# Half-width tap matrices on TensorE and a reordered opening in a fused convolution and feed-forward kernel

## The chip, the cores and the metric

The kernel runs on one core of one Trainium2 chip. The metric is the device time of one launch in microseconds. Before the change the median of 9 runs is 699.56 us (698.77 to 700.28).

## The reference

A depthwise causal convolution of 7 taps along the sequence, with softmax-normalised taps for each of 8 heads, is followed by a feed-forward layer with a leaky ReLU. Cut to what matters:

```python
# x: (8, 4096, 192) float32, weight: (8, 7), w_in: (192, 2048), w_out: (2048, 192)
w = np.exp(weight - np.max(weight, axis=-1, keepdims=True))
w = w / (np.sum(w, axis=-1, keepdims=True) + 1e-09)
x_pad = np.concatenate([np.zeros((B, 6, D)), x], axis=1)
out = np.einsum('hk,bskhg->bshg', w, x_unf)   # x_unf[b, s, k] = x_pad[b, s + k], 24 columns per head
h = out.reshape(B * S, D) @ w_in
y = np.maximum(0.01 * h, h) @ w_out           # (32768, 192) float32
```

## The kernel before

**Tiling.** Two batch rows (e = 0, 1) are worked on together. A block is 512 positions of both rows; there are 32 blocks. The 192 columns are cut into three chunks of 64. A tile such as xt or yt holds, for each chunk, 64 columns of row 0 on partitions 0 to 63 and 64 columns of row 1 on partitions 64 to 127, and positions along the free axis. The first five blocks are worked on in halves of 256 positions, ten of them ("half 0" to "half 9"), and the other blocks whole. The list `groups` (lines 64 and 65) holds these ten halves and then the blocks.

**Bringing x in.** The first four halves come by SyncE in float32 (load_first, tile x_nat, two buffers), are cast to bf16 (cast_first, tile x_bf), transposed on TensorE (transpose_first, two tiles ptr in PSUM) and copied out of PSUM (evac_first) into xt. The later blocks come by load_x (six cast DMAs on GpSimd's queue into x_bf, three buffers) and transpose_x (three transposing DMAs on SyncE's queue).

**The convolution.** VectorE does it with one TENSOR_SCALAR (line 168) and six SCALAR_TENSOR_TENSOR (line 174) for each chunk, giving yt. For chunks 0 and 1 of halves 0 and 1 TensorE does it in its place (pe_conv_jobs, line 190): for each tap a diagonal matrix of the tap weights, in two parts (a bf16 value and the rest), is multiplied with the shifted xt and summed in a PSUM tile acc; the sum is scaled by the softmax's denominator on the way out. The diagonal matrices (tile diag, 128 by 128) are made by VectorE (the high part, line 274) and ScalarE (the low part, line 282).

**The two products.** mm1 multiplies yt with 128 columns of w_in at a time into ph (PSUM pool with 2 buffers of two banks), and ScalarE applies the leaky ReLU into g (line 348). A step j of a half is two such u. The second product is cut into slots, of which mm2_slot works one: each slot is one 128-row chunk of w_out for one unit of 128 positions of one row, half of its rows now and the other half LAG = 24 slots later. So unit n starts in slot 16n, is complete in slot 16n + 39, and is then copied out by evac_o (line 400) and stored by SyncE, two units at a time.

**PSUM.** The tiles ptr, acc and po share one tag of a pool with 4 buffers of one bank each.

**The order.** The kernel is written under a manual schedule: on each engine and each queue the instructions stand in the order of the program. The main loop runs over the groups i; within it the steps j: two mm1, then `quota` slots of the second product (none in half 0, 16 in each step of half 1 and later halves), then the convolution instructions of the next group (`ahead`), and then what stands at special places. Before the main loop stand the loads of weights, the softmax of the taps, the warming products (warm, line 236, on zeros), the tap matrices and the convolution of half 0. These lines set the places of halves 1 to 3:

```python
if i == 0 and u == 1:            # half 1: transposes and copies, then the conv of half 1
    transpose_first(1)
...
if i < 2 and j == 3:
    transpose_first(i + 2)
    evac_first(i + 2, nc.vector.tensor_copy, nc.vector.tensor_copy)
```

Of the kernel before, what the change touches and what calls it, by code (L numbers as in the profile page):

```python
# [9 lines left out]
FP32 = mybir.dt.float32  # L10
BF16 = mybir.dt.bfloat16
# [3 lines left out]
def kernel(  # L15
# [8 lines left out]
    nc = tc.nc  # L24
# [10 lines left out]
    CH = 64  # L35
# [34 lines left out]
    def load_x(blk):  # L70

        if blk >= NBLK:
            return
        rp, st = divmod(blk, NB)
        t = xb_pool.tile([128, NCH, SUB, 2, CH], BF16, name="x_bf")
        src = x[:, st * ST : (st + 1) * ST, :].rearrange("r (s p) d -> r p s d", p=128)
        for c in range(NCH):
            for e in range(2):
                nc.gpsimd.dma_start(  # L79
                    out=t[:, c, :, e, :],  # L80
                    in_=src[2 * rp + e, :, :, c * CH : (c + 1) * CH],
                )
# [21 lines left out]

    def load_first(q):
        t = stage_pool.tile([128, 2, HS, D], FP32, name="x_nat")
        for e in range(2):
            nc.sync.dma_start(  # L110
                out=t[:, e, :, :],
                in_=x[e, q * HT : (q + 1) * HT, :].rearrange("(c p) d -> p c d", p=128),
            )
        x_nat[q] = t

    def cast_first(q, e, copy):
# [27 lines left out]
    def evac_first(q, *copies):  # L144
        dst = xt[0][:, :, HALO + q * HT : HALO + (q + 1) * HT].rearrange(
            "p c (s i k) -> p i s c k", s=HS, i=2
        )
        for i, t in enumerate(ptr.pop(q)):
            copies[i](out=dst[:, i], in_=t)  # L149
# [4 lines left out]
    def conv_jobs(grp, chunks=range(NCH)):  # L154
        blk, t0, T = grp
        rp, st = divmod(blk, NB)
        if blk not in yt:
            yt[blk] = yt_pool.tile([128, NCH, ST], BF16, name="yt")
        y = yt[blk]
        jobs = []  # L160
        for c in chunks:
            for k in range(K):
                a = BASE + k + st * ST + t0
                src = xt[rp][:, c, a : a + T]
                dst = y[:, c, t0 : t0 + T]
                if k == 0:
                    jobs.append(
                        lambda s=src, d=dst, c=c: nc.vector.tensor_scalar_mul(  # L168
                            d, s, wk[:, c, 0:1]
                        )  # L170
                    )
                else:
                    jobs.append(
                        lambda s=src, d=dst, c=c, k=k: nc.vector.scalar_tensor_tensor(  # L174
                            out=d, in0=s, scalar=wk[:, c, k : k + 1], in1=d,
                            op0=mybir.AluOpType.mult, op1=mybir.AluOpType.add,
                        )
                    )
        return jobs

    def pe_conv_jobs(grp, c):


        blk, t0, T = grp
        acc = psum_o.tile([128, ST], FP32, name="acc", tag="po")
        jobs = []
        for p in range(2):
            for k in range(K):
                jobs.append(
                    lambda k=k, p=p: nc.tensor.matmul(  # L190
                        out=acc[:, :T], lhsT=diag[c][:, p, k, :],
                        rhs=xt[0][:, c, BASE + k + blk * ST + t0 : BASE + k + blk * ST + t0 + T],
                        start=(k == 0 and p == 0), stop=(k == K - 1 and p == 1),
                    )
                )
        return jobs, lambda scale: scale(yt[blk][:, c, t0 : t0 + T], acc[:, :T], rsum[:, c, :])  # L196


# [8 lines left out]
    nc.vector.memset(junk, 0.0)  # L207
    ident = const_pool.tile([128, 128], BF16)
    make_identity(nc, ident)

    sel = const_pool.tile([H, NCH, 2, CH], FP32, name="sel")
    nc.gpsimd.memset(sel, 1.0)  # L212
# [21 lines left out]
    def warm(n):  # L234
        for _ in range(n):
            nc.tensor.matmul(  # L236
                out=wa[:, 0, 0:HT], lhsT=zero[:, 0:128], rhs=zero, start=True, stop=True
            )
# [9 lines left out]
        out=w9[:, 0:K], in_=w9[:, 0:K], func=mybir.ActivationFunctionType.Exp,  # L248
        bias=nmax, scale=1.0, accum_out=w9[:, K : K + 1],
    )  # L250
    warm(7)
    wps = psum_h.tile([128, 2, ST], FP32, name="wps", tag="ph")
    for c in range(NCH):
        nc.tensor.matmul(
# [7 lines left out]
    cast_first(0, 1, nc.scalar.copy)  # L262

    wraw = wps[:, 0, 0 : NCH * (K + 1)].rearrange("p (c k) -> p c k", c=NCH)
    wkh = const_pool.tile([128, NCH, K], BF16, name="wkh")
    wkl = const_pool.tile([128, NCH, K], FP32, name="wkl")
    nc.vector.tensor_copy(out=wkh, in_=wraw[:, :, 0:K])
    nc.vector.tensor_sub(wkl, wraw[:, :, 0:K], wkh)


    diag = [const_pool.tile([128, 2, K, 128], BF16, name=f"diag{c}") for c in range(NPEC)]

    def diag_high(c):
        nc.vector.tensor_mul(  # L274
            diag[c][:, 0],
            ident[:, None, :].to_broadcast([128, K, 128]),
            wkh[:, c, :, None].to_broadcast([128, K, 128]),
        )

    def diag_low(c, ks):  # L280
        for k in ks:
            nc.scalar.activation(  # L282
                out=diag[c][:, 1, k, :], in_=ident,
                func=mybir.ActivationFunctionType.Copy, scale=wkl[:, c, k : k + 1],
            )

    transpose_first(0)
    warm(3)
    diag_high(0)
    diag_low(0, range(2))  # L290
    evac_first(0, nc.vector.tensor_copy, nc.scalar.copy)
    diag_low(0, range(2, K))
    diag_high(1)
    diag_low(1, range(K))
    rsum = const_pool.tile([128, NCH, 1], FP32)
# [7 lines left out]
            out=out, in_=in_, func=mybir.ActivationFunctionType.Copy, scale=scale  # L303
        )

    load_first(2)
    for job in conv_jobs(groups[0], range(NPEC, NCH)):
        job()
    for c in range(NPEC):
# [5 lines left out]
    cast_first(1, 0, nc.vector.tensor_copy)  # L315
    cast_first(1, 1, nc.vector.tensor_copy)
    load_first(3)
    load_x(2)
    transpose_x(2)


    g, po, osb, seal = {}, {}, {}, {}
# [70 lines left out]
    def evac_o(n):  # L393
# [7 lines left out]
        if n % 2 == 1:  # L401
# [3 lines left out]
                in_=osb.pop(n // 2),  # L405
            )

    slot, avail = 0, 0
    for i, grp in enumerate(groups):
        blk, t0, T = grp  # L410
        steps = T // 64
        if t0 == 0:
            g[blk] = g_pool.tile([128, NFC, 2, ST], BF16, name="g", tag="g")
        quota = (avail - slot) // steps

        if i == 0:
            ahead, pe_ahead = [], []
# [81 lines left out]
```

## Time and profile before

| | us |
|---|---|
| median of 9 runs | 699.56 |
| the profiled execution, device time | 698.8 |
| its span, first to last instruction | 697.1 |
| TensorE busy (share of the span) | 689.7 (99%) |
| VectorE busy | 540.3 (78%) |
| ScalarE busy | 512.2 (73%) |
| GpSimd busy | 142.0 (20%) |
| VectorE's SCALAR_TENSOR_TENSOR rows of the convolution | 439.5 |
| TensorE's tap products (56) | 7.6 |
| ScalarE's low tap matrices (14) | 4.3 |
| VectorE's high tap matrices (2) | 2.2 |

Busy times come from one profiled execution. Matmuls overlap, and their ends are modelled, so a busy TensorE is not TensorE at its peak. In the timelines a row gives the start, the length, the engine (PE is TensorE, PEld its weight loads, DVE VectorE, ACT ScalarE, POOL GpSimd, SP SyncE; a q after it means its queue), the line, the operation, the tile written and those read, the shapes and the count; in brackets stands how long the engine was idle before it and what ended that.

### The profile page before, as it was taken

To read this page: it belongs to the slowest core of one execution; us is meant where nothing else is said; L and a number is where in the kernel's file an instruction comes from. 1 tells how busy PE (TensorE), PEld (TensorE's weight loads), DVE (VectorE), ACT (ScalarE), POOL (GpSimd) and SP (SyncE) were. 2 spreads that over 40 slices of the span, in tenths; PEclk is the share of its full clock that TensorE was granted. 3 is DMA by queue.
4 is the path that set the end of the run, shared out by engine and by line. 5 is a ranking of instruction groups with operands and counts; after the bars stand their busy time and mean duration, and the time that the engine had idled before them with its cause. 6 is when DMAs were issued, how large, how long until landed. Compare 5 with 4: busy or idle time off the path is not lost.

```text
span 697.1 us, 25946 instructions
## 1 busy us (share of the span) xinstructions
PE 689.7 (99%) x11730; PEld 611.7 (88%) x11730; DVE 540.3 (78%) x995; ACT 512.2 (73%) x574; POOL 142.0 (20%) x198
## 2 busy tenths in 40 slices
PE   9999999999999999999999999999999999999997
PEld 6899998678888888888888888888888888888887
DVE  6799999967777787777787777787777787777712
ACT  6788887977777777777777777777777777777770
POOL 6432221420222211222220222211222210000000
PEclk9999999999999999999999999999999999999999
DMA  9986653855556635557644556525555535112112
GB/s 177 129 93 74 83 84 70 91 71 81 73 66 93 81 65 87 66 74 93 79 75 78 70 72 89 85 64 82 73 75 84 87 67 76 55 51 59 47 36 69
DMA packets 184847, 54.37 MB, mean 78 GB/s; under 512 B 148385, under 2 KB 184737, under 8 KB 184737
## 3 DMA queue, kind: packets, MB, share of 16 engines
q0 software_dynamic: 98768, 14.17, 29.4%
q1 hardware_dynamic: 85968, 38.56, 22.7%
q8 instruction: 91, 1.49, 0.9%
q14 instruction: 20, 0.16, 0.1%
HBM read 29.88 MB, written 25.17 MB: 79 GB/s over the span
## 4 chain that ended last, share of the span: by engine, by line
PE 89%; DVE 6%; DMA 3%; issue 0%; ACT 0%; POOL 0%; POOLq 0%; ACTq 0%
PE po L361 46%; PE ph L341 44%; DVE yt L174 6%; DMA w_out<-in_moe_w_out_dram 2%; DMA w_in<-in_moe_w_in_dram 1%; DVE yt L168 0%; ACT g L348 0%; POOL sel L214 0%; DVE xt L149 0%; POOL sel L212 0%; PE ptr L135 0%; DVE o_sb L400 0%; POOL ident masks.py:199 0%; ACT o_sb L400 0%; POOL ident masks.py:197 0%
## 5 line engine op out<-in xcount | busy, mean ns | idle before, releaser
L348 ACT ACTIVATE g<-ph 128x1024 bf16<-128x1024 f32 x512 | 496.2, 1021 | 165.3 <-PE ph L341 165.3
L174 DVE SCALAR_TENSOR_TENSOR yt<-xt,wk,yt 128x512 bf16<-128x512 bf16 (+1 forms) x642 | 439.5, 685 | 17.4
L361 PE MATMUL po<-w_out,g 64*128 64x192 bf16 (+1 forms) x8048 | 397.8, 243 | 0.2 <-DMA w_out<-in_moe_w_out_dram 0.2
L361 PEld LDWEIGHTS <-g 64*128 64x128 bf16 (+1 forms) x8048 | 372.1, 94 | 28.9 <-issue 0.5
L341 PE MATMUL ph<-yt,w_in 64*128 64x512 bf16 (+1 forms) x3552 | 391.9, 347 | 2.0 <-DVE yt L174 1.1
L341 PEld LDWEIGHTS <-w_in 64*128 64x128 bf16 x3552 | 249.1, 94 | 47.5 <-issue 5.3
L79 POOL DMA_DIRECT2D x_bf<-in_x_dram x180 | 133.6, 771 | 432.8 <-DMA xt<-x_bf 424.4
L400 DVE COPY o_sb<-po 128x192 f32<-128x192 f32 x216 | 77.2, 357 | 127.4 <-PE po L361 124.9
L168 DVE TENSOR_SCALAR yt<-xt,wk 128x512 bf16<-128x512 bf16 (+1 forms) x107 | 35.9, 335 | 0.2
L400 ACT COPY o_sb<-po 128x192 f32<-128x192 f32 x40 | 13.0, 325 | 0.0
L190 PE MATMUL acc<-xt,diag 128*128 128x256 bf16 x56 | 7.6, 293 | 0.0
L190 PEld LDWEIGHTS <-diag 128*128 128x128 bf16 x56 | 5.7, 104 | 1.7 <-issue 0.4
L236 PE MATMUL warm<-zero 128*128 128x256 bf16 x20 | 4.5, 372 | 1.1 <-DVE junk L207 1.1
L224 POOL DMA_DIRECT2D w_in<-in_moe_w_in_dram x8 | 5.1, 644 | 0.0
L282 ACT ACTIVATE diag<-ident,wkl 128x128 bf16<-128x128 bf16 x14 | 4.3, 389 | 0.1
L149 DVE COPY xt<-ptr 128x384 bf16<-128x384 bf16 x7 | 2.2, 353 | 2.4 <-PE ptr L135 2.4
L236 PEld LDWEIGHTS <-zero 128*128 128x128 bf16 x20 | 2.2, 122 | 1.8 <-DVE junk L207 1.1
L120 DVE CAST x_bf<-x_nat 128x384 bf16<-128x384 f32 x7 | 2.7, 414 | 1.4 <-DMA x_nat<-in_x_dram 1.4
L196 DVE TENSOR_SCALAR yt<-acc,rsum 128x256 bf16<-128x256 f32 x2 | 1.0, 480 | 2.3 <-PE acc L190 2.3
L274 DVE TENSOR_TENSOR diag<-ident,wkh 128x896 bf16<-128x896 bf16 x2 | 2.2, 1081 | 0.0
L135 PEld LDWEIGHTS <-x_bf 64*128 64x128 bf16 x48 | 1.2, 101 | 0.9 <-issue 0.8
L135 PE MATMUL ptr<-ident,x_bf 64*128 64x64 bf16 x48 | 1.7, 202 | 0.2 <-ACT o_sb L400 0.2
(27 smaller groups left out, 11.8 us busy)
## 6 DMA issues: line engine op xcount, KB each, us to landing
out_dram<-o_sb SPq DMA_DIRECT2D x128, 192.0 KB, 2.1
x_bf<-in_x_dram POOLq DMA_DIRECT2D x180, 64.0 KB, 3.4
x_nat<-in_x_dram SPq DMA_DIRECT2D x8, 192.0 KB, 6.1
w_in<-in_moe_w_in_dram POOLq DMA_DIRECT2D x8, 192.0 KB, 8.8
xt<-x_bf SPq DMA_TRANSPOSE x90, 2.4
w_out<-in_moe_w_out_dram POOLq DMA_DIRECT2D x1, 768.0 KB, 14.5
w<-in_weight_dram SPq DMA_DIRECT2D x1, 0.2 KB
```

The costliest lines, as they stand in the source:

```text
L79: nc.gpsimd.dma_start(out=t[:, c, :, e, :], in_=src[2 * rp + e, :, :, c * CH : (c + 1) * CH],)
L135: nc.tensor.transpose(out=ts[i][:, s, c, :], in_=x_bf[q // 2][ps, c, (q % 2) * HS + s, :, :].rearrange("p e k -> p (e k)"), identity=ident ...
L168: lambda s=src, d=dst, c=c: nc.vector.tensor_scalar_mul(d, s, wk[:, c, 0:1])
L174: lambda s=src, d=dst, c=c, k=k: nc.vector.scalar_tensor_tensor(out=d, in0=s, scalar=wk[:, c, k : k + 1], in1=d, op0=mybir.AluOpType.mult, ...
L190: lambda k=k, p=p: nc.tensor.matmul(out=acc[:, :T], lhsT=diag[c][:, p, k, :], rhs=xt[0][:, c, BASE + k + blk * ST + t0 : BASE + k + blk * ...
L224: nc.gpsimd.dma_start(out=w_in[e * CH : (e + 1) * CH, :, fs], in_=moe_w_in[:, fs].rearrange("(c p) f -> p c f", p=CH),)
L236: nc.tensor.matmul(out=wa[:, 0, 0:HT], lhsT=zero[:, 0:128], rhs=zero, start=True, stop=True)
L282: nc.scalar.activation(out=diag[c][:, 1, k, :], in_=ident, func=mybir.ActivationFunctionType.Copy, scale=wkl[:, c, k : k + 1],)
L341: nc.tensor.matmul(out=ph[:, e, i * T : (i + 1) * T], lhsT=w_in[ps, c, f * 128 : (f + 1) * 128], rhs=y[ps, c, t0 : t0 + T], start=(c == 0) ...
L348: act = nc.scalar.activation(out=g[blk][:, nf * u : nf * (u + 1), :, t0 : t0 + T], in_=ph.rearrange("p e (i t) -> p i e t", i=nf), func=my ...
L361: ins = nc.tensor.matmul(out=po[m], lhsT=g[b][ps, fc, e, s * 128 : (s + 1) * 128], rhs=w_out[ps, fc, :], start=(rt != 1 and fc == 0), stop ...
L400: copy(out=o_sb[:, n % 2, :], in_=po.pop(n))
```

## The change

The tap matrices are folded from 128 by 128 to 128 by 64: the identity's two diagonal blocks are added into one 128 by 64 tile, ident2, and each tap product becomes two products of 64 by 64, one for the lower and one for the upper partitions, which write the lower and the upper partitions of the same acc. wkh and wkl are made for the two chunks that TensorE may do only. There are two more warming products before wps and one more after the transposes of half 0. In half 1 TensorE does chunk 0 only; VectorE does chunks 1 and 2. The casts of halves 2 and 3 move from VectorE to ScalarE, among the activations of halves 0 and 1. The load of half 2 waits for the last low tap matrix of chunk 0. The load and the transposing DMAs of block 2 move from before the main loop into it, the load behind a one-element copy on GpSimd that reads the last g of half 0. The transposes and copies of half 2 keep their place in half 0's last step, but stand before the convolution instructions, of which there are none left there; the transposes of half 3 move from half 1's step 3 to step 1, while their copies stay in step 3.

```diff
-    def load_first(q):
+    def load_first(q, after=None):
...
-            nc.sync.dma_start(
+            ins = nc.sync.dma_start(
...
+            if after is not None and e == 0:
+                tc.add_manual_dep(
+                    ins.ins, after.ins.name,
...
+                    reason="leave the DMA engines to w_in",
+                )
@@ pe_conv_jobs
         for p in range(2):
             for k in range(K):
-                jobs.append(
-                    lambda k=k, p=p: nc.tensor.matmul(
-                        out=acc[:, :T], lhsT=diag[c][:, p, k, :],
-                        rhs=xt[0][:, c, BASE + k + blk * ST + t0 : BASE + k + blk * ST + t0 + T],
-                        start=(k == 0 and p == 0), stop=(k == K - 1 and p == 1),
+                a = BASE + k + blk * ST + t0
+                for e in range(2):
+                    ps = slice(e * CH, (e + 1) * CH)
+                    jobs.append(
+                        lambda k=k, p=p, a=a, e=e, ps=ps: nc.tensor.matmul(
+                            out=acc[ps, :T], lhsT=diag[c][ps, p, k, :],
+                            rhs=xt[0][ps, c, a : a + T],
+                            start=(k == 0 and p == 0), stop=(k == K - 1 and p == 1),
+                        )
                     )
-                )
@@ setup
+    ident2 = const_pool.tile([128, CH], BF16)
+    nc.vector.tensor_add(ident2, ident[:, 0:CH], ident[:, CH:128])
...
-    warm(7)
+    warm(9)
...
-    wkh = const_pool.tile([128, NCH, K], BF16, name="wkh")
-    wkl = const_pool.tile([128, NCH, K], FP32, name="wkl")
+    wkh = const_pool.tile([128, NPEC, K], BF16, name="wkh")
+    wkl = const_pool.tile([128, NPEC, K], FP32, name="wkl")
...
-    diag = [const_pool.tile([128, 2, K, 128], BF16, name=f"diag{c}") for c in range(NPEC)]
+    diag = [const_pool.tile([128, 2, K, CH], BF16, name=f"diag{c}") for c in range(NPEC)]
...
     transpose_first(0)
-    warm(3)
+    warm(4)
     diag_high(0)
     diag_low(0, range(2))
     evac_first(0, nc.vector.tensor_copy, nc.scalar.copy)
-    diag_low(0, range(2, K))
+    low = diag_low(0, range(2, K))
...
-    load_first(2)
+    load_first(2, low)
...
     load_first(3)
-    load_x(2)
-    transpose_x(2)
@@ main loop
+    pjunk = const_pool.tile([1, 1], BF16)
...
                 if i == 0 and u == 1:
                     transpose_first(1)
                     evac_first(1, nc.vector.tensor_copy, nc.vector.tensor_copy)
-                    ahead = conv_jobs(groups[1], range(NPEC, NCH))
-                    evacs = []
-                    for c in range(NPEC):
-                        pe_jobs, evac_y = pe_conv_jobs(groups[1], c)
-                        pe_ahead += pe_jobs
-                        evacs.append(evac_y)
+                    pe_ahead, evac_y = pe_conv_jobs(groups[1], 0)
+                    ahead = conv_jobs(groups[1], range(1, NCH))
                     per = len(ahead)
-                if i == 0 and u in (3, 5):
-                    for job in pe_ahead[: 2 * K]:
+                if i == 0 and u == 3:
+                    for job in pe_ahead:
                         job()
-                    pe_ahead = pe_ahead[2 * K :]
+                if i == 0 and u in (5, 6):
+                    cast_first(2, u - 5, nc.scalar.copy)
+                if i == 1 and u in (0, 2):
+                    cast_first(3, u // 2, nc.scalar.copy)
             for _ in range(quota):
                 mm2_slot(slot)
                 slot += 1
+            if i == 0 and j == 3:
+                evac_y(nc.vector.tensor_scalar_mul)
+                transpose_first(2)
+                evac_first(2, nc.vector.tensor_copy, nc.vector.tensor_copy)
+            if i == 1 and j == 1:
+
+                nc.gpsimd.tensor_copy(out=pjunk, in_=g[0][0:1, NFC - 1, 1, HT - 1 : HT])
+                load_x(2)
+            if i == 2 and j == 1:
+                transpose_x(2)
             for job in ahead[per * j : per * (j + 1)]:
                 job()
-            if i == 0 and j == 2:
-                for evac_y in evacs:
-                    evac_y(nc.vector.tensor_scalar_mul)
-                for e in range(2):
-                    cast_first(2, e, nc.vector.tensor_copy)
-            if i == 1 and j == 2:
-                for e in range(2):
-                    cast_first(3, e, nc.vector.tensor_copy)
-            if i < 2 and j == 3:
-
-                transpose_first(i + 2)
-                evac_first(i + 2, nc.vector.tensor_copy, nc.vector.tensor_copy)
+            if i == 1 and j == 1:
+                transpose_first(3)
+            if i == 1 and j == 3:
+                evac_first(3, nc.vector.tensor_copy, nc.vector.tensor_copy)
```

More of the change, by code (lines that the diff above doesn't have):

```diff
@@ L113, in load_first @@
             )
+            if after is not None and e == 0:
+                tc.add_manual_dep(
+                    ins.ins, after.ins.name,
+                    mybir.DependencyInfo(
+                        mybir.DependencyClass.Sync, mybir.DependencyReason.DATA
+                    ),
+                    reason="leave the DMA engines to w_in",
+                )
         x_nat[q] = t
@@ L264 @@
     wraw = wps[:, 0, 0 : NCH * (K + 1)].rearrange("p (c k) -> p c k", c=NCH)
-    wkh = const_pool.tile([128, NCH, K], BF16, name="wkh")
-    wkl = const_pool.tile([128, NCH, K], FP32, name="wkl")
-    nc.vector.tensor_copy(out=wkh, in_=wraw[:, :, 0:K])
-    nc.vector.tensor_sub(wkl, wraw[:, :, 0:K], wkh)
-    diag = [const_pool.tile([128, 2, K, 128], BF16, name=f"diag{c}") for c in range(NPEC)]
+    wkh = const_pool.tile([128, NPEC, K], BF16, name="wkh")
+    wkl = const_pool.tile([128, NPEC, K], FP32, name="wkl")
+    nc.vector.tensor_copy(out=wkh, in_=wraw[:, 0:NPEC, 0:K])
+    nc.vector.tensor_sub(wkl, wraw[:, 0:NPEC, 0:K], wkh)
+    diag = [const_pool.tile([128, 2, K, CH], BF16, name=f"diag{c}") for c in range(NPEC)]
     def diag_high(c):
@@ L275, in diag_high @@
             diag[c][:, 0],
-            ident[:, None, :].to_broadcast([128, K, 128]),
-            wkh[:, c, :, None].to_broadcast([128, K, 128]),
+            ident2[:, None, :].to_broadcast([128, K, CH]),
+            wkh[:, c, :, None].to_broadcast([128, K, CH]),
         )
@@ L281, in diag_low @@
         for k in ks:
-            nc.scalar.activation(
-                out=diag[c][:, 1, k, :], in_=ident,
+            act = nc.scalar.activation(
+                out=diag[c][:, 1, k, :], in_=ident2,
                 func=mybir.ActivationFunctionType.Copy, scale=wkl[:, c, k : k + 1],
             )
+        return act
     transpose_first(0)
-    warm(3)
+    warm(4)
     diag_high(0)
@@ L416 @@
         if i == 0:
-            ahead, pe_ahead = [], []
+            ahead = []
         else:
```

## The prediction

> **What bounds the kernel now.** I read the totals first, then the chain that ended last, then each engine's timeline around the places where that chain changes engine.
>
> ```profile
> PE 689.7 (99%) x11730; PEld 611.7 (88%) x11730; DVE 540.3 (78%) x995; ACT 512.2 (73%) x574; POOL 142.0 (20%) x198
> ...
> PE 89%; DVE 6%; DMA 3%; issue 0%; ACT 0%; POOL 0%; POOLq 0%; ACTq 0%
> ```
>
> TensorE is full over the span, so what the opening loses is never made up. But 6% of the chain lies on VectorE, and the chain over 60 to 140 us (columns: start, length, what) says where:
>
> ```profile
> 83.76 0.67 PE ph L341 x12
> 84.43 0.29 DVE yt L168
> ...
> 118.65 0.76 DVE yt L174
> 119.42 0.04 issue
> 119.46 1.04 PE ph L341 x8
> ```
>
> TensorE's timeline shows the same place: the first full block waits 1.08 us for its third chunk.
>
> ```profile
> 117.77 0.61 PE L341 MATMUL ph<-yt,w_in 64*128 64x512 bf16 x4
> 119.46 1.04 PE L341 MATMUL ph<-yt,w_in 64*128 64x512 bf16 x8 [1.08 <-DVE yt L174]
> ```
>
> VectorE's timeline says how far back that goes. From 34.15 us on it has no gap: seven half-block convolutions of 9.97 us (three chunks of 3.33) and one block of 15.0. It is let go there by TensorE's transposes of half 3:
>
> ```profile
> 33.50 0.62 DVE L149 COPY xt<-ptr 128x384 bf16<-128x384 bf16 x2 [0.95 <-PE ptr L135]
> 34.15 0.29 DVE L168 TENSOR_SCALAR yt<-xt,wk 128x256 bf16<-128x256 bf16 x1
> ```
>
> So two clocks meet at 119.46: VectorE from 34.15, and TensorE, which does a half in 10.52 us (33.30 to 43.82). After that TensorE alone decides. TensorE in the stretch that the change rearranges, where each row is one step's product or its second product (x32 are 16 slots):
>
> ```profile
> 28.74 1.50 PE L361 MATMUL po<-w_out,g 64*128 64x192 bf16 x32
> 30.06 1.49 PE L341 MATMUL ph<-yt,w_in 64*128 64x256 bf16 x24
> 31.37 1.50 PE L361 MATMUL po<-w_out,g 64*128 64x192 bf16 x32
> 32.71 0.19 PE L135 MATMUL ptr<-ident,x_bf 64*128 64x64 bf16 x1
> 33.14 0.33 PE L135 MATMUL ptr<-ident,x_bf 64*128 64x64 bf16 x11 [0.24 <-ACT o_sb L400]
> 33.30 1.48 PE L341 MATMUL ph<-yt,w_in 64*128 64x256 bf16 x24
> ```
>
> The transposes already waited 0.24 us for an output copy: they take buffers from the same four as the output sums. That wait is the clue to what follows.
>
> **What the Trainium skill says.** "PSUM — Partial Sum Buffer", Specifications, gives 8 banks of 2 KiB. The pool ph takes 2 x 2 of them and po the other 4, so a fifth live po tile has nowhere to go; the 0.24 us agrees. "TensorEngine Tiling (Array Packing)", Gotcha 1, says that different row tiles cannot access one bank at the same time, while the PSUM page (The four PSUM rules) calls groups in different quadrants of a bank independent. The new tap products do exactly that, and no row of this trace shows it: row pairs here write two banks. "TensorE: Matmul & The Clock Gate", Part 1, halves the clock after an idle window of about 3.4 us. The trace has the cold pace (7 warming products from 1.13 us step by 0.21 us, the 14 of 9.12 us by 0.11) though its clock row reads full.
>
> **Part by part: the head (0 to 11 us).** One more warming product before the first tap product moves it from 6.44 to 6.60 us; the two more before wps fill a gap of 0.19 and cost under 0.05. At 0.213 us cold and 0.109 warm the 28 tap steps then end 0.11 later. Tap steps become pairs of 64x64 products; I take a pair at the old step's price, as the row pairs of L341 run (24 in 1.31 us, 0.055 each). Below that I see no gain, since each pair streams the same 256 columns; above, each product alone costs 0.11. First product: 11.08 -> 11.19. The half-width matrices save VectorE about 0.46 each (1.08 us for 896 columns), the first lost again in waiting for the transposes. ScalarE's 14 narrow scalings step by 0.29; from "ScalarE: Activation LUTs", What ACT_TABLE_LOAD costs (0.83 ns an element), I estimate 0.24, so 0.7 less. Both hidden: TensorE's tap steps end last. The new add (ident2) fits VectorE's 1.10 us wait for w. Narrower wkh, wkl: under 0.02.
>
> **Half 0 (11.2 to 22 us).** TensorE loses 14 of 28 tap steps (1.65 us), but does not own the time. ScalarE steps by 0.92 us: its eight g rows stood at 12.14, 14.37, 17.43 and 20.50 us in pairs, with two waits of 1.12 us behind the tap products.
>
> ```profile
> 17.43 1.94 ACT L348 ACTIVATE g<-ph 128x1024 bf16<-128x1024 f32 x2 [1.12 <-PE ph L341]
> 20.50 3.88 ACT L348 ACTIVATE g<-ph 128x1024 bf16<-128x1024 f32 x4 [1.12 <-PE ph L341]
> ```
>
> One wait goes; two casts come (0.51 us each on ScalarE). New: u4 at 17.55, u5 18.46, cast 19.40, u6 19.83, cast 20.77 to 21.28, u7 21.2 to 22.2. The transposes of half 2 need both casts: TensorE at 21.36 (was 20.95), VectorE's copies at 21.73, and its conv of half 2 starts at 22.38 (was 21.97). VectorE's extra chunk (3.33 us), less an evacuation (0.40) and the casts (0.74), fits its old waits of 2.31 and 0.45: it is done by 20.8. So half 1's first product stays at 21.65, half 1 running on to about 32.5 if nothing stops it.
>
> **Loads.** load_first(2), two SP issues, moves from about 5 to 7.6 us; at the 6 to 9 us such loads took it lands by 17, before its cast at 19.4. load_first(3), behind it on SP, waits for half 1's casts as before. load_x(2), six POOL issues of 0.74, moves from 10.1 to about 22.3 behind the new one-element copy; load_x(3), behind it, ends near 31 instead of 27.5, and is not needed until half 3. I cost these at nothing: VectorE does not read block 2 until 43 us. If w_in or w_out comes earlier, that lands ahead of the stall below, which swallows it. The three transposing DMAs of load 2 move from 24.40 to behind the second output store on SP.
>
> **Half 1: the new wait.** Now the transposes of half 3 go out after step 1 (slots 0 to 31), their copies only after all 21 conv instructions of half 2. At slot 32 product unit 2 needs a po buffer. Unit 0 holds one until slot 39, unit 1 until slot 55, the two ptr tiles hold the others: none is free. TensorE waits for VectorE's first copy of half 3. It arrives at slot 32 at 28.55: 22.9 (u7's g, u1's product) + four rows of 1.315 + transposes 0.35 + one row of 1.315, less overlap. VectorE ends half 2 at 22.38 + 9.98 = 32.36, copies by 32.64, TensorE resumes at 32.70: **4.15 us idle**. Queued behind it are the rest of half 1 and all of half 2; ScalarE runs dry. Half 2 starts at 32.70 + 3 x 1.315 = 36.65 (was 33.30), and the first full block at 36.65 + 8 x 10.52 = 120.81. Its third chunk would be due at 121.24, against 119.46: **+1.78 us**. The old slack (1.08 there, 0.3 at 43.8, 0.24 at 33) has paid the rest.
>
> VectorE is next in line. Half 3 runs 33.0 to 43.0; half 4 needs the DMA transposes. The second store followed the start of half 2 by 5.67 us (38.97), so now 42.3, transposes from 42.75, landing 2.4 to 4.6 later. VectorE starts half 4 at 45.2 to 47.3, and its last chunk ends 74.8 us on, at 120.0 to 122.1. Early landing leaves TensorE the bound, late landing adds up to 0.9.
>
> **The sum.** 1.8 us. The profiled execution took 698.8 us for a span of 697.1, so about 700.6; it was the second fastest of the nine runs, 0.76 below their median of 699.56. Against the median: **701.4**. About 0.2% (1.4 us) is what a measurement of this kernel can tell.
>
> **Rivals.**
> - *No buffer wait* (faster). If the queue order let VectorE copy half 3 before TensorE reaches slot 32 (the deciding point is 28.55 us), half 2 starts at 32.5, VectorE's gapless run at 33.0 instead of 34.15 and ends at 117.8: -1.6, 698.0. For it: the casts off VectorE are worth 2 x 0.74. Against: the copies stand after conv work worth 9.98 us. It is also what comes out if the buffers are counted otherwise than I count.
> - *The stall cools the clock.* An idle of 4.15 us can hold a whole window of 3.4: one or two windows at half pace cost 1.7 to 3.4 more, some 703.9. For it: the cold start. Against: only about a fifth of positions fit.
> - *Quadrants do not overlap.* Then 28 tap products cost 0.11 each: half 0 starts 2.9 us later and its own chunk costs 1.5 more; half 3's copies shift by 4.4: 705.8. Against: the quadrant sentence above.
> - *The change does less*: the head warms earlier, or landings differ; between 699.3 and 700.8.
>
> **Numbers.** Stall as computed 0.65 (own range 700.7 to 702.4), cooled clock 0.10, quadrants 0.06, no wait 0.13, in between 0.06. The likeliest gives 701.4. The range 699.3 to 704.6 leaves out the faster rival and the quadrants. Of the forecast case, about a fifth could fall within 0.2%: faster 0.14, same 0.18, slower 0.68.
>
> **What would show it.** TensorE idle some 4 us near 28.5 before a po product, released by VectorE's copy (xt); ptr of half 3 long before its copy; a VectorE gap near 43 to 46 for the DMA transposes; the 1.08 us wait at the first full block gone; L190 as 84 products in pairs near 0.11. If that idle is absent, I am wrong on the sign; if pairs step by 0.2 warm, on the size.

## The result, and the profile after

The kernel with the change takes 704.6 us in the median of 10 runs (702.5 to 706.91), the kernel before 699.45 us in the median of the 31 runs that it is compared with. The ratio is 1.0076, with a 95% interval of 1.0068 to 1.0084: slower, by 5.15 us. The forecast was 701.4 us, 1.84 above the median it started from. The sign and the main mechanism are as forecast; the size is nearly three times as large. The profiled execution of the changed kernel took 705.5 us for a span of 703.7, against 698.8 and 697.1 before.

The totals, and the chain of work that ended last:

```profile
PE 691.0 (98%) x11761; PEld 613.4 (87%) x11761; DVE 542.1 (77%) x998; ACT 513.1 (73%) x578; POOL 142.2 (20%) x199
...
PE 89%; DVE 9%; ACT 1%; issue 1%; ACTq 0%
```

TensorE is busy for 1.3 us more than before, in a span that is 6.6 us longer: most of the loss is time in which TensorE stood. VectorE's share of the chain went from 6% to 9%, so the chain still passes through the convolution. TensorE's timeline shows where (start, length, what; in brackets the idle time before and its releaser):

```profile
12.60 1.58 PE L354 MATMUL ph<-yt,w_in 64*128 64x256 bf16 x24
...
28.23 1.49 PE L354 MATMUL ph<-yt,w_in 64*128 64x256 bf16 x24
34.65 2.75 PE L374 MATMUL po<-w_out,g 64*128 64x192 bf16 x32 [4.93 <-DVE xt L157]
37.16 1.64 PE L354 MATMUL ph<-yt,w_in 64*128 64x256 bf16 x24
38.62 1.50 PE L374 MATMUL po<-w_out,g 64*128 64x192 bf16 x32
39.94 1.49 PE L354 MATMUL ph<-yt,w_in 64*128 64x256 bf16 x24
```

The 4.93 us are the forecast wait: a second product, released by VectorE's copy of half 3 out of PSUM. Two things are not in the forecast. The row after the wait takes 2.75 us for the work that its neighbours do in 1.50, and half 2 (39.94) starts 6.64 us later than before, where 3.35 were forecast.

The stages view of the same place has the reason for the slow row (columns: stretch, its length, busy time and count of PE, PEld, DVE, ACT and POOL, granted clock, DMA share, GB/s):

```profile
30.00:34.00 4.00, 0.00 (x0) 0.00 (x0) 3.75 (x9) 1.05 (x2) 4.00 (x7) 1.00 1.44 90
34.00:37.20 3.20, 2.55 (x34) 2.55 (x35) 3.06 (x7) 0.32 (x1) 3.07 (x5) 0.51 1.38 87
37.20:40.00 2.80, 2.80 (x62) 2.76 (x58) 2.62 (x7) 1.82 (x2) 0.00 (x0) 0.95 0.81 54
```

While TensorE is idle the granted clock still reads 1.00; in the 3.2 us after it is 0.51. The wait cooled the clock.

VectorE's timeline holds the other two terms:

```profile
23.59 0.29 DVE L176 TENSOR_SCALAR yt<-xt,wk 128x256 bf16<-128x256 bf16 x1
...
26.92 0.57 DVE L176 TENSOR_SCALAR yt<-xt,wk 128x256 bf16<-128x256 bf16 x1
...
30.54 0.66 DVE L176 TENSOR_SCALAR yt<-xt,wk 128x256 bf16<-128x256 bf16 x1
...
34.24 0.61 DVE L157 COPY xt<-ptr 128x384 bf16<-128x384 bf16 x2
34.89 0.75 DVE L176 TENSOR_SCALAR yt<-xt,wk 128x256 bf16<-128x256 bf16 x1
...
50.38 0.29 DVE L176 TENSOR_SCALAR yt<-xt,wk 128x256 bf16<-128x256 bf16 x1 [4.97 <-DMA xt<-x_bf]
```

The first instruction of a chunk, 0.28 or 0.29 us where GpSimd issues nothing, takes 0.57, 0.66 and 0.75 here. The convolution of half 2 (23.59 to 34.24) therefore takes 10.65 us instead of 9.98, and the copies that TensorE waits for stand behind it. Beside these instructions GpSimd issues 18 loads, the moved one of block 2 and those of blocks 3 and 4 behind it, for 13.35 us without a gap:

```profile
23.72 13.35 POOL L79 DMA_DIRECT2D x_bf<-in_x_dram  x18
```

At 50.38 VectorE has waited 4.97 us for the transposing DMAs of block 2:

```profile
46.11 5.40 SPq L94 DMA_TRANSPOSE xt<-x_bf  x3
```

They stand on SyncE behind an output store that follows TensorE's progress, were issued from 46.11, and the first took 4.25 us to land. From there VectorE runs without a gap, and it ends later than TensorE at the first full block:

```profile
124.10 0.64 PE L354 MATMUL ph<-yt,w_in 64*128 64x512 bf16 x4
125.79 1.04 PE L354 MATMUL ph<-yt,w_in 64*128 64x512 bf16 x8 [1.04 <-DVE yt L182]
```

So TensorE loses 4.93 us and a slow row at 30 to 37, and 1.04 us once more at 125, because the same delay reached VectorE by way of the store and the DMA then landed late.

### The profile page after: what moved, and what is told of

It is laid out like the page before. It is cut to its first block, busy times and chain, and to the rows that moved or that the text cites. A ratio compares the mean times of both kernels' runs of the same rounds, so it can differ in the third digit from the quotient of the medians.

```text
span 703.7 us, 26013 instructions
## 1 busy us (share of the span) xinstructions
PE 691.0 (98%) x11761; PEld 613.4 (87%) x11761; DVE 542.1 (77%) x998; ACT 513.1 (73%) x578; POOL 142.2 (20%) x199
## 4 chain that ended last, share of the span: by engine, by line
PE 89%; DVE 9%; ACT 1%; issue 1%; ACTq 0%
PE po L374 44%; PE ph L354 42%; DVE yt L182 8%; ACT g L361 1%; PE acc L201 1%; DVE yt L176 1%; PE warm L250 1%; PE wps L268 0%; DVE xt L157 0%; PE ptr L143 0%; ACT x_bf L128 0%; DVE o_sb L413 0%; DVE zero L216 0%; DVE junk L218 0%; ACTq L413 0%
## 5 line engine op out<-in xcount | busy, mean ns | idle before, releaser
L176 DVE TENSOR_SCALAR yt<-xt,wk 128x512 bf16<-128x512 bf16 (+1 forms) x108 | 37.4, 346 | 5.2 <-DMA xt<-x_bf 5.0
L201 PE MATMUL acc<-xt,diag 64*64 64x256 bf16 x84 | 6.6, 319 | 0.0
L201 PEld LDWEIGHTS <-diag 64*64 64x64 bf16 x84 | 5.2, 126 | 1.3 <-issue 0.6
L296 ACT ACTIVATE diag<-ident,wkl 128x64 bf16<-128x64 bf16 x14 | 3.6, 336 | 0.2 <-DVE wkl L282 0.2
L128 ACT CAST x_bf<-x_nat 128x384 bf16<-128x384 f32 x5 | 2.6, 511 | 1.5 <-DMA x_nat<-in_x_dram 1.5
```

Source lines behind the costliest of these rows:

```text
L176: lambda s=src, d=dst, c=c: nc.vector.tensor_scalar_mul(d, s, wk[:, c, 0:1])
L201: lambda k=k, p=p, a=a, e=e, ps=ps: nc.tensor.matmul(out=acc[ps, :T], lhsT=diag[c][ps, p, k, :], rhs=xt[0][ps, c, a : a + T], start=(k == ...
L296: act = nc.scalar.activation(out=diag[c][:, 1, k, :], in_=ident2, func=mybir.ActivationFunctionType.Copy, scale=wkl[:, c, k : k + 1],)
```

## The experiments

Each ratio is to the kernel before, run on the same chip at the same time, with its 95% interval; it is not the quotient of the two medians, and can differ from it by some 0.0005. Theory A is the forecast's: the copies of half 3 come too late, and the buffers they hold stop TensorE. Theory B blames the first 11 us (the head), theory C the late load of block 2.

### The copies of half 3 behind their transposes

In the changed kernel:

```diff
             if i == 1 and j == 1:
                 transpose_first(3)
-            if i == 1 and j == 3:
                 evac_first(3, nc.vector.tensor_copy, nc.vector.tensor_copy)
```

> The changed kernel with one line moved: VectorE's copies of half 3 follow TensorE's transposes of it in step 1 and no longer stand in step 3. Theory A (the buffer wait is the cause, and the cooled clock and the late transposing DMAs follow from it): TensorE's 4.9 us wait at slot 32 shrinks under 1 us, the half-pace row after it goes, half 2 starts near 34 instead of 39.94, the DMA transposes of block 2 leave 5 to 6 us earlier, and VectorE's wait of 4.97 us for them falls under 1. VectorE then runs gapless from 34.3, 10 us a half: 75.4 us after about 44.5 us, against 125.72 now: 5 to 5.5 us less, so within 0.7 us of the kernel before. Theory B (the head is the cause: narrow tap products on a clock that stays cold longer): 1.4 us of the loss stays at most where A takes it all, and the 4.9 us wait was slack that VectorE would have cost anyway: 703 to 704.6. Theory C (the late load of block 2 is the cause): the wait of VectorE near 45 to 50 us stays at 4 us or more, and the time stays above 703.

Measured: 699.13 us, ratio 0.9996 (0.9987 to 1.0004). Moving two copies gives back all of the 5.15 us and a little more. TensorE's timeline of this kernel:

```profile
28.11 1.49 PE L354 MATMUL ph<-yt,w_in 64*128 64x256 bf16 x24
29.43 1.50 PE L374 MATMUL po<-w_out,g 64*128 64x192 bf16 x32
...
119.11 1.04 PE L354 MATMUL ph<-yt,w_in 64*128 64x512 bf16 x8 [0.92 <-DVE yt L182]
```

The second product follows the first with no wait and no slow row. The transposing DMAs go out 6.56 us sooner (39.55 instead of 46.11), so VectorE has no gap. The fold, the casts on ScalarE and the moved load are all still in this kernel, and it is level with the kernel before. That they cost nothing does not follow: the kernel before with nothing but half 3's casts, transposes and copies moved early is faster still (the last but one experiment).

### The split of transposes and copies alone, in the kernel before

```diff
+                if i == 1 and u in (0, 2):
+                    cast_first(3, u // 2, nc.scalar.copy)
...
-            if i == 1 and j == 2:
-                for e in range(2):
-                    cast_first(3, e, nc.vector.tensor_copy)
-            if i < 2 and j == 3:
-                transpose_first(i + 2)
-                evac_first(i + 2, nc.vector.tensor_copy, nc.vector.tensor_copy)
+            if i == 0 and j == 3:
+                transpose_first(2)
+                evac_first(2, nc.vector.tensor_copy, nc.vector.tensor_copy)
+            if i == 1 and j == 1:
+                transpose_first(3)
+            if i == 1 and j == 3:
+                evac_first(3, nc.vector.tensor_copy, nc.vector.tensor_copy)
```

> The kernel before, with TensorE's transposes of half 3 in step 1 of half 1 and VectorE's copies left in step 3; to allow it, the two casts of half 3 go to ScalarE in steps 0 and 1. Taps stay full width, load and DMA transposes of block 2 stay early. Theory A: the buffer wait appears by itself, about 3 us (slot 32 reached near 29.1, half 2 convolved at 21.97 + 9.98, first copy done at 32.3); half 2 starts 3 us later than 33.30, the old slack of 1.4 to 1.7 is used up, and the time is 1.3 to 1.8 us over the kernel before; 1.4 more if the clock cools (idle of 3 us may be too short). Theory B or C: the head and the load are those of before, so the time is that of before, within 0.5 us, or less, since two casts leave VectorE.

Measured: 702.9 us, ratio 1.0051 (1.0038 to 1.0064), some 3.5 us, where A gave 2.7 to 3.2 with a cooled clock. The split alone makes the wait and the slow rows:

```profile
33.07 2.74 PE L361 MATMUL po<-w_out,g 64*128 64x192 bf16 x32 [3.69 <-DVE xt L149]
35.58 1.93 PE L341 MATMUL ph<-yt,w_in 64*128 64x256 bf16 x24
37.34 1.49 PE L361 MATMUL po<-w_out,g 64*128 64x192 bf16 x32
38.66 1.48 PE L341 MATMUL ph<-yt,w_in 64*128 64x256 bf16 x24
```

An idle of 3.69 us cools the clock too: these two rows take 1.70 us more than two warm ones. At the first full block (122.82) TensorE does not wait for VectorE, and half 2 starts 1.28 us sooner than in the changed kernel (38.66 against 39.94): these two are what its trace lacks of the changed kernel's loss.

### The same wait with TensorE kept busy

In the changed kernel, 34 products of zeros fill most of the wait:

```diff
+            if i == 1 and j == 2:
+                wb = psum_h.tile([128, 2, ST], FP32, name="warm2", tag="ph")
+                for _ in range(34):
+                    nc.tensor.matmul(
+                        out=wb[:, 0, 0:HT], lhsT=zero[:, 0:128], rhs=zero, start=True, stop=True
+                    )
             for _ in range(quota):
                 mm2_slot(slot)
```

> The changed kernel with 34 products of zeros on TensorE (0.109 us each, 3.7 us in all, into a free ph buffer that nobody reads) ahead of slot 32 in half 1, so that the wait for VectorE's copy is filled. Theory A1 (the idle stretch cools the clock, and that is a part of the loss by itself): the rows after the wait run at full pace (1.32 us instead of 2.75), half 2 starts 1.3 to 1.7 us earlier than 39.94, the DMA transposes and VectorE's half 4 follow, and the time is 1.2 to 1.7 us below the changed kernel: 702.9 to 703.4. Rival (the slow rows are not the clock's doing, or VectorE's chain hides them): 704 to 705, slow rows still there or no gain from their going.

Measured: 702.28 us, ratio 1.0041 (1.0028 to 1.0053). The useful work is the same and TensorE is let go at nearly the same time; the clock differs:

```profile
30.36 3.87 PE L454 MATMUL warm<-zero 128*128 128x256 bf16 x34 [0.47 <-ACT g L361]
34.75 1.50 PE L374 MATMUL po<-w_out,g 64*128 64x192 bf16 x32 [0.52 <-DVE xt L157]
```

The stages view of the same stretch as above:

```profile
34.00:37.20 3.20, 2.68 (x57) 2.54 (x56) 3.02 (x8) 0.58 (x2) 3.19 (x5) 1.00 1.37 87
```

The second product starts 0.10 us later than in the changed kernel, but takes 1.50 us and not 2.75, at a clock of 1.00. So the cooling cost some 2.3 us (704.6 - 702.28; the two intervals leave about 1 us either way), more than expected. In the traces half 2 starts 1.24 us sooner (38.70), the output store and the DMAs behind it move with it (44.87 instead of 46.11), and the 1.04 us at the first full block are gone. The last is not the clock's alone: the first of these DMAs landed in 3.17 us here and in 4.25 there. The changed kernel's own runs agree. In ten of eleven, the profiled one among them, the mean granted clock was 0.995 to 0.998; the one at 1.000 took 702.5 us.

### A shorter wait

In the changed kernel, the copies of half 3 after 15 of the 21 convolution instructions of half 2:

```diff
-            for job in ahead[per * j : per * (j + 1)]:
+            for n, job in enumerate(ahead[per * j : per * (j + 1)]):
+                if i == 1 and j == 2 and n == 3:
+                    evac_first(3, nc.vector.tensor_copy, nc.vector.tensor_copy)
                 job()
...
-            if i == 1 and j == 3:
-                evac_first(3, nc.vector.tensor_copy, nc.vector.tensor_copy)
```

> The changed kernel with VectorE's copies of half 3 after 15 of the 21 convolution instructions of half 2 instead of after all 21. Theory A: the copy comes 6 instructions or some 3 us sooner, so TensorE's wait falls from 4.9 to about 2 us. If the clock cools only after more than 3 us of idle (it did at 3.7 to 4.9), the slow rows go as well; half 2 starts near 36, and the DMA transposes on SyncE move with it, so the time lies 2 to 3 us over the kernel before: 701.4 to 702.4. If it cools after 2 us too: 702.5 to 703.5. Rival (the wait passes into the time only above the slack of about 1.5 us that TensorE has against VectorE, and nothing else follows from it): 700 to 700.6.

Measured: 700.12 us, ratio 1.0006 (0.9998 to 1.0014).

```profile
30.93 1.50 PE L374 MATMUL po<-w_out,g 64*128 64x192 bf16 x32 [1.43 <-DVE xt L157]
```

An idle of 1.43 us leaves the row at 1.50: no cooling. I had put the copies too late, so A's numbers missed. The time fits the rival's, yet VectorE did wait for the DMAs, by 1.08 us, which the rival left out. What the run gives is a dose: against the copies placed at once, 1.43 us of wait cost 0.7 (by the ratios) to 1.0 us (by the medians), with intervals that overlap, and 4.93 us cost 5.5.

### The load of block 2 back in its place

In the changed kernel load_x(2) and transpose_x(2) stand before the main loop again, as before the change:

```diff
+    load_x(2)
+    transpose_x(2)
...
-    pjunk = const_pool.tile([1, 1], BF16)
...
-            if i == 1 and j == 1:
-                nc.gpsimd.tensor_copy(out=pjunk, in_=g[0][0:1, NFC - 1, 1, HT - 1 : HT])
-                load_x(2)
-            if i == 2 and j == 1:
-                transpose_x(2)
```

> The changed kernel with the load and the DMA transposes of block 2 back before the main loop, without the one-element copy. Theory A: the wait at slot 32 stays, only a little shorter because GpSimd no longer issues 18 loads beside VectorE's half 2 (its first rows of a chunk took 0.57 to 0.66 instead of 0.28: 0.7 us); VectorE's 4.97 us wait for the transposes goes, and TensorE's own lateness binds (third chunk due at 124.5 instead of 125.8): 1.3 to 2 us less than the changed kernel, 702.6 to 703.3. Theory C: all of the loss goes, 699.5 to 700.5. Theory B: no change against the changed kernel, 704 to 705.

Measured: 703.36 us, ratio 1.0057 (1.0044 to 1.0069), 1.2 us better than the change. VectorE's wait for the DMAs of block 2 is gone and the first full block starts without one; the wait for the copies stays, at 4.24 us and cooled:

```profile
34.19 2.48 PE L376 MATMUL po<-w_out,g 64*128 64x192 bf16 x32 [4.24 <-DVE xt L157]
...
123.96 1.48 PE L356 MATMUL ph<-yt,w_in 64*128 64x512 bf16 x12
```

VectorE's chunks of half 2 begin with 0.29, 0.28 and 0.28 us, and two of half 3 with 0.59 and 0.65 beside GpSimd's next loads. But the chunk at 27.15 also stood beside GpSimd's issues (24.28 to 27.99), and so did one of the kernel before:

```profile
23.74 3.71 POOL L79 DMA_DIRECT2D x_bf<-in_x_dram  x5 [3.80 <-DMA w_out<-in_moe_w_out_dram]
...
25.30 0.28 DVE L168 TENSOR_SCALAR yt<-xt,wk 128x256 bf16<-128x256 bf16 x1
```

So standing beside an issue is not enough; the last section has what decides. With the copies early as well, both edits in one kernel:

> The changed kernel with both repairs: VectorE's copies of half 3 right behind the transposes in step 1, and the load and the DMA transposes of block 2 back before the main loop. Without the buffer wait VectorE decides at the first full block (its third chunk waited 0.92 us in the kernel with the copies alone moved). Theory A (the late load has a small price of its own: first rows of a chunk at 0.57 to 0.75 us instead of 0.28 while GpSimd issues 18 loads, some 0.6 us of VectorE's chain): 0.3 to 0.8 us below that kernel, 698.3 to 698.8. Rival (the late load is free, or early loads take the DMA engines from w_in, as the change's own text says): 699 to 700.

Measured: 698.77 us, ratio 0.9993 (0.9985 to 1.0001). That is 0.36 us under the kernel with the copies alone, and the intervals overlap widely: inconclusive. The late load, its issues and its place behind the store together, costs 1.2 us where the wait delays that store, and nothing that can be told where it does not.

### The fold, undone and alone

The tap matrices at 128 by 128 again in the changed kernel, and at half width in the kernel before; the core of the second edit, the first is its reverse:

```diff
-                jobs.append(
-                    lambda k=k, p=p: nc.tensor.matmul(
-                        out=acc[:, :T], lhsT=diag[c][:, p, k, :],
+                for e in range(2):
+                    ps = slice(e * CH, (e + 1) * CH)
+                    jobs.append(
+                        lambda k=k, p=p, a=a, e=e, ps=ps: nc.tensor.matmul(
+                            out=acc[ps, :T], lhsT=diag[c][ps, p, k, :],
...
-    diag = [const_pool.tile([128, 2, K, 128], BF16, name=f"diag{c}") for c in range(NPEC)]
+    diag = [const_pool.tile([128, 2, K, CH], BF16, name=f"diag{c}") for c in range(NPEC)]
```

> The changed kernel with its tap matrices 128 wide again and one full product for each tap step; everything else as changed. Theory A: the head is not where the time went; the clock warmed late in the traced execution by the place of its window, not because the products are narrow, so over several runs this is within 0.7 us of the changed kernel (704 to 705), and the 4.9 us wait stays. Theory B: full products warm the clock by 8.2 us as in the kernel before; half 0 starts near 11.2 instead of 12.6, all that follows to VectorE's chain moves by 1.4, and the time is 703.0 to 703.4. If the head were the whole cause: 699.5 to 700.

Measured: 704.49 us, ratio 1.0069 (1.0056 to 1.0083), no different from the change. The wait and the half-paced rows are there too. The fold is not the cause.

```profile
35.02 1.97 PE L369 MATMUL po<-w_out,g 64*128 64x192 bf16 x32 [4.01 <-DVE xt L157]
36.76 2.73 PE L349 MATMUL ph<-yt,w_in 64*128 64x256 bf16 x24
```

> The kernel before with nothing but the folded tap matrices: 64 columns wide, each tap step two products in diagonal quadrants, two chunks in both halves. Theory A: a pair takes the time of one full product, VectorE and ScalarE save about 1 us of making the matrices, but TensorE's tap steps end the head, so it is the time of before within 0.5 us. Theory B: the narrow products keep the clock cold longer (the tap stretch of half 0 took 3.19 us in two traces of the changed kernel and 2.13 in a third, 2.5 to 3.0 with full products): 0.5 to 1.5 us slower.

Measured: 699.73 us, ratio 1.0003 (0.9995 to 1.0012). On TensorE's timeline a pair of quadrants runs at one full product's price, as the prediction took it:

```profile
10.30 1.72 PE L193 MATMUL acc<-xt,diag 64*64 64x256 bf16 x28
```

These are 14 tap steps in pairs, all at the warm clock; 14 full-width products took 1.70 us.

### Transposes and copies early, in the kernel before

The experiments point to what of the change pays: the casts of half 3 on ScalarE, and its transposes in step 1 with the copies beside them. The edit is that of the split alone, except that the copies stay with the transposes:

```diff
             if i == 1 and j == 1:
                 transpose_first(3)
-            if i == 1 and j == 3:
                 evac_first(3, nc.vector.tensor_copy, nc.vector.tensor_copy)
```

> The kernel before, with the casts of half 3 on ScalarE in steps 0 and 1 of half 1, TensorE's transposes of it in step 1 and VectorE's copies right behind them; full-width taps and the early load of block 2 as before. Theory A: no buffer wait, and VectorE's gapless run loses the 0.95 us wait for the transposes and two casts of 0.74 in all; it would bring the third chunk of the first full block 1.7 us earlier, where TensorE, due at 118.2, binds: 1.0 to 1.4 us faster than the kernel before, 698.0 to 698.5. Rival (the step-1 transposes cost TensorE a wait for buffers or VectorE's copies are late there too): 699.5 or more.

Measured over 20 runs: 697.78 us (697.1 to 699.34), ratio 0.9979 (0.9973 to 0.9986). It beats both kernels. Its first full block:

```profile
118.86 1.04 PE L341 MATMUL ph<-yt,w_in 64*128 64x512 bf16 x8 [0.40 <-DVE yt L174]
```

VectorE starts half 3 without the gap it had at 33 us, and the wait of 1.08 us of before is down to 0.40.

Two comparisons are cleaner than those with the kernel before. The split alone differs from this kernel only in where the copies stand: 702.9 against 697.78 us, with half 2 at 38.66 against 33.67, so the late copies cost some 5.0 us by the ratios. And the changed kernel with its copies at once has all of this edit and the rest of the change: at 0.9996 it is some 1.2 us slower, and the intervals do not meet; with block 2's load early as well (0.9993) it is still some 1.0 us slower, with intervals that just touch. So something in the rest of the change costs about 1 us (the warming products, the casts and the load of half 2, chunk 1 of half 1 on VectorE, or the fold, which alone showed no cost); these runs do not show which.

Last, in the kernel with the copies at once, TensorE's tap products for chunks 0 and 1 of half 1, as before the change:

```diff
-                    pe_ahead, evac_y = pe_conv_jobs(groups[1], 0)
-                    ahead = conv_jobs(groups[1], range(1, NCH))
+                    ahead = conv_jobs(groups[1], range(NPEC, NCH))
+                    pe_ahead, evacs = [], []
+                    for c in range(NPEC):
+                        pe_jobs, evac_y = pe_conv_jobs(groups[1], c)
+                        pe_ahead += pe_jobs
+                        evacs.append(evac_y)
...
```

> The changed kernel with the copies of half 3 right behind the transposes, and in half 1 both chunks 0 and 1 on TensorE again, 28 products behind u3 and 28 behind u5 as in the kernel before. Theory A: VectorE gains 3 us in half 0 that it cannot use, since half 2's transposes wait for ScalarE's second cast, and that stands behind the activation of u6, which now comes after the second tap stretch: half 1 and VectorE's half 2 start 1.0 to 1.5 us later, 700 to 700.7. Rival (VectorE's work is what counts): half 2 starts earlier and the time is 0.5 to 1 us below the kernel with the copies alone moved, 698.2 to 698.7.

Measured: 699.89 us, ratio 1.0008 (1.0001 to 1.0014), some 0.8 us slower than with one chunk, with intervals that just overlap. VectorE stands idle for 2.13 us before half 2, and its copies of half 2 come 0.6 us later (22.66 against 22.05): in this arrangement, with the casts of half 2 on ScalarE, giving chunk 1 to VectorE was sound.

## Why the prediction was right on the sign and wrong on the size

**Right.**
- No po buffer was free at slot 32, and the first copy of half 3 released TensorE. Forecast 4.15 us, measured 4.93. The copies at once remove it; the split alone makes it.
- Against the kernel before, only part of a delay there reaches the end, since VectorE set the end there and TensorE had time to spare: the split alone held half 2 back to 38.66, 5.36 us later than before, and cost 3.5.
- The pairs of quadrants overlap. "TensorEngine Tiling (Array Packing)", Gotcha 1, would have them exclude each other within one bank; here they did not, with 28 products in 1.72 us. The PSUM page's sentence on quadrants is about sums that are open at once and says nothing of time; the time is shown by these runs.
- VectorE's gap for the transposing DMAs came, though later than forecast. ScalarE's narrow scalings step by 0.24 us as estimated (12 in 2.96 us; 3.61 before).

**Wrong.** The forecast had the third chunk of the first full block due at 121.24 us; its products started at 125.79. The excess of 4.55 us, by the steps:

| step | forecast | measured | excess, us |
|---|---|---|---|
| VectorE starts half 2 | 22.38 | 23.59 | 1.21 |
| VectorE works on half 2 | 9.98 | 10.65 | 0.67 |
| last copy to TensorE's start | 0.34 | 0.41 | 0.07 |
| rows from the wait to half 2 (36.65 - 32.70; 39.94 - 34.65) | 3.95 | 5.29 | 1.34 |
| the third chunk after TensorE could take it (124.10 + 0.43) | 0 | 1.26 | 1.26 |

- *The clock* was the step that failed. "Only about a fifth of positions fit" gave it a chance of 0.10; it happened in ten of eleven runs. All four traces with an idle of 3.69 to 4.93 us show rows at half pace, and those with 1.43 us, or with the wait filled, do not. The estimate let the window of 3.4 us lie anywhere and counted how often it fits whole into 4.15; four of four traces do not look like that. "TensorE: Matmul & The Clock Gate", Why this matters for your kernels, advises against gaps of over about 3 us without a word on position, and these runs agree as far as they go: idles of 3.69 us and more cooled, 1.43 did not. Its price, some 2.3 us by the filled wait, is within the rival's 1.7 to 3.4.
- *"I cost these at nothing"* of the loads was wrong twice. "VectorE does not read block 2 until 43 us" looked at who needs the data and not at what the issues do to others. "SBUF — State Buffer", Who interferes with whom, says that a tensor_scalar in a two-port mode and GpSimd can block each other. The traces agree as far as they go: such instructions take up to 0.75 us when they meet one of GpSimd's issues at the wrong moment and 0.28 or 0.29 where it issues nothing, and SCALAR_TENSOR_TENSOR stays at 0.485 us. That it is this lock was not tried. In the last row of the table the DMAs landed at the slow end, which the forecast had priced at "up to 0.9" and taken as 0; they also left 3.4 us later, with the delayed store. The load in its old place gives back 1.2 us.
- *The head* was taken from one trace that warmed early: first product at 11.08 us before, 12.60 after. Of this, 0.46 us is fixed: the first tap product stands at 6.90 or 6.91 in all seven half-width traces of the changed kernel, against 6.44 before and a forecast of 6.60. The rest varies from execution to execution: the first 14 tap steps took 2.52 to 3.14 us in four traces at full width and 2.05 to 3.19 in eight at half width. The fold's own runs show no cost, though a cost of up to 0.8 us lies within the interval of the kernel with the fold alone. VectorE starts half 2 at 22.71 to 23.98 us in seven traces with the change's half 1, and at 21.97 to 23.18 in the four with that of before. The trace of before is the earliest of its four, so the 1.21 us in the table's first row are mostly the forecast's starting point; on medians, the step from 700.6 to 701.4 may already have paid for 0.76 of it.
- *Three sums* do not come out. For slot 32 the forecast adds four rows of 1.315, 0.35 and one more row to 22.9, which makes 29.8; its 28.55 needs three rows. TensorE in fact fell idle at 29.72. VectorE's work from half 4 to its last chunk is given as 74.8 us, but the trace of before has 75.2 (44.21 to 119.41). And the two warming products before wps were priced at under 0.05; they move what follows by 0.17 (the transposes of half 0 start at 5.51 instead of 5.34).

On medians: 701.4 forecast, 702.28 with the clock kept warm, 704.6 as it is. The clock is some 2.3 of the 3.2 us that are missing. VectorE's longer half 2, 0.67, is near the rest of 0.9, but was not isolated, and the cost of about 1 us in the rest of the change is as near.

## What to carry to other kernels

A transpose through PSUM holds its buffer until its copy has run: move both or neither, and count the live buffers at the slot where the next sum asks for one. When a change makes TensorE idle for as long as it was here (3.7 us or more; between 1.43 and 3.69 nothing was tried), price the cooled clock as the likely case and add it to the wait, with whatever follows TensorE's progress, such as stores and the transfers queued behind them. A transfer that nobody needs yet can still cost: look at what runs beside its issue, and at what stands ahead of it in its queue. And when a change of many parts comes out level, it may hold a gain and a loss: build the gain alone.

## What the runs showed of the hardware that I had not expected

- TensorE cooled after idles of 3.69, 4.01, 4.24 and 4.93 us in every trace, and not after 1.43. Nothing between was tried. The clock row reads 1.00 in the idle stretch and 0.51 in the one after it, so the cooling is read from the stretch that follows. In the first 10 us the row reads 1.00 although the products run at the cold pace.
- VectorE's TENSOR_SCALAR on 256 bf16 columns took 0.28 or 0.29 us in all 205 cases, over the twelve traces, in which GpSimd issued nothing beside it. In 103 cases it overlapped an issue of x (0.74 to 0.92 us each). The moment decides: of the 53 that began 0.20 to 0.52 us after the issue did, 50 were lengthened, to as much as 0.67 us, and ended 0.77 to 0.91 after its start; of the other 50 only one was, the 0.75 us at 34.89.
- The first of the changed kernel's three transposing DMAs of block 2 took 2.79 us to issue and 4.25 to land; the other two issued in 1.2 and landed in 2.4. The next three, behind an output store as well, issued in 1.2 to 1.3 and landed in up to 5.2. What makes one of them slow, these runs do not show.
